# Three query and key buffers, and attention's load buffers laid out as whole weight tiles

## The chip, the cores and the metric

The kernel runs on one core of a Trainium2 chip. The metric is device time in microseconds (us) of one execution; three timed executions of the kernel before gave a median of 371.08 us, and one more was profiled. The names of the engines are those of the profile: PE is the matrix engine, DVE, ACT and POOL are the vector, scalar and general engines, SP is the queue from which nearly every load is issued.

## The reference

Three layers follow each other. Attention over 4 batches, 8 heads, 576 positions and a head size of 64, where a head sees only the last 32 positions (heads 0 to 3) or every 32nd position (heads 4 to 7):

```python
scores = scale * np.matmul(q, k.transpose(0, 1, 3, 2))
scores = np.where(masks[None, :, :, :], scores, -1000000000.0)
attn = softmax(scores);  x = (attn @ v) as 2304 x 512
```

A mixture of 8 experts over 32 slots (4 per expert), with a softmax over all 2304 tokens into the slots and one over the slots out of them:

```python
logits = x @ phi;  d = softmax(logits, axis=0);  slot_input = d.T @ x
slot_out[e] = np.maximum(slot_input[e] @ w1[e], 0) @ w2[e]      # w1: 512x1024, w2: 1024x512
x = softmax(logits, axis=1) @ slot_out
```

And a gated layer: `(silu(x @ w_gate) * (x @ w_val)) @ w_out`, with 1536 hidden units. Its three weights are float64 bit patterns that the kernel converts itself.

## The kernel before, in words

**Attention** is done in 16 units (two batches of one head each), every unit in three steps, 48 steps. The loop goes through them two at a time: in the pass for steps n and n+1 it issues the score products of both (`qk`, L290), the products with v of the steps four back (`pv`, L328), the transposes of the steps two back (`tr`, L315, copied by ACT at L318), and the exponentials (`expo`, ACT at L308) of the two. Transposes of the finished x (L353), the logits (L373) and, for the first eight units, the slot sums (L438) stand between them. Every engine runs its instructions in exactly this written order.

**Loads** go out on SP's queue in written order. Queries and keys of a unit are two loads (`load_qk`, L259 and L260), its values one (`load_v`, L268), after which POOL copies parts of the values (L271). Each has two buffers (`AHEAD = 2`): the pair for unit u+2 is issued after unit u's last score product is issued, the values for u+2 after the last product of unit u with its values. SP waits, in order, for the last reader of the buffer. A table, `WSCHED`, says how many weight halves (128x1024, 512 KB) are issued after each unit by `load_half` (L178). At most eight loads are on their way: every load also waits for the landing of the one eight places ahead of it, and `order` shows that wait by the name of one of eight counters, DMAHW0 to DMAHW7, taken in turn.

**Weights.** There are 70 halves: six of the gated layer's (`PRE`, converted during attention, L194 to L208), 32 of w1 (16 tiles of two halves, tile 2e+h for expert e) and 32 of w2 (tiles 16 to 31). A ring of 15 whole tiles (`NB = 15`, pool `wp`) takes most of them. When attention is over its load buffers (pool `ld`) are given up as a whole, and three further tiles (`wp2`) and the slot input `sz` are placed there. The tiles in `SPEC` and `SPLIT` go into attention's own x buffers and work space as these come free.

**After attention** come the slot sums' rest, then w1 (L644, 16 tiles, in the order `W1ORDER`, each freed ring tile taking the next w2 tile), the hidden units, and w2 (L733, 16 tiles, in the order `W2ORDER`). At the end of w2 the pools are closed and a new pool `fr` is laid over the same memory: four buffers `g` for the gated layer's next weights (`load_g`, L674), the split output weights and the accumulators. A new buffer waits for the last use of every old tile that it covers.

**The gated layer** starts with two prepared weight tiles. Its opening (`HEAD`) is written out by hand: products with tile 0 (`a0`), then ACT takes the first half of the next gate tile from its `g` buffer (L224), then the rest. The long tail is its output products (L840).

Of the kernel before, what the change touches and what calls it, by code (L numbers as in the profile page):

```python
# [17 lines left out]
S = 576  # L18
HD = 64
NT = 9  # L20
# [7 lines left out]
NB = 15  # L28
NB2 = 3
# [3 lines left out]
WORDER = list(range(1, 13)) + list(W2ORDER[:6]) + list(SPEC) + [SPLIT] + list(W2ORDER[6:])  # L33
W1ORDER = (1, 2, 3, 4, 5, 6, 0, 7, 14, 8, 15, 9, 10, 13, 12, 11)
# [22 lines left out]
WSCHED = [2, 2, 2, 2, 2, 2, 2, 2, 2, 2, 5, 3, 2, 2, 1, 2, 3]  # L57
# [4 lines left out]
AHEAD = 2  # L62
# [48 lines left out]
def build(ctx: ExitStack, tc: tile.TileContext, cst, phi, qh, kh, vh, w1, w2, wgv, wo, out):  # L111
# [10 lines left out]
    es_ld = ExitStack()  # L122
    lp = es_ld.enter_context(tc.tile_pool(name="ld", bufs=1, side="right"))
# [15 lines left out]
    qt, kt, vt = [], [], []  # L139
    for j in range(AHEAD):  # L140
        qt.append(lp.tile([128, S], F32, name=f"q{j}"))
        kt.append(lp.tile([128, PAD + S], F32, name=f"k{j}"))
        vt.append(lp.tile([96, 2 * NT * (HD + 1)], F32, name=f"v{j}"))
    col = lp.tile([128, 128], F32, name="col")
    par = lp.tile([128, 16], F32, name="par")
    ml = lp.tile([128, 192], F32, name="ml")
    ms = lp.tile([128, 720], F32, name="ms")

    wsrc = [w1[j] for j in range(16)] + [w2[j] for j in range(16)]
    loads = [(j, hf) for j in PRE + WORDER for hf in range(2)]  # L150
    loads.remove((SPEC[0], 0))
    loads.insert(2 * (NB + len(PRE)), (SPEC[0], 0))
    loads.remove((SPLIT, 0))
    loads.insert(2 * (NB + len(PRE) + NB2) + 1, (SPLIT, 0))
# [4 lines left out]
    def load_half(k, pool=wp, bufs=NB):  # L159
        for _ in range(k):  # L160
# [3 lines left out]
            if j in SPEC:  # L164
                wt[j, hf] = (ap_.tile([128, 1024], F32, tag="xT", name="wx", bufs=1) if hf and j == SPEC[0] else
                             ap_.tile([128, 1024], F32, tag="x", name="wx", bufs=5))
            elif j == SPLIT:
                wt[j, hf] = ap_.tile([128, 1024], F32, tag="eT", name="wx", bufs=1) if hf else tmp[:, 0:1024]
# [10 lines left out]
            wn[0] += 1  # L179

# [75 lines left out]
    def load_qk(u):  # L256
        if u >= 16:
            return
        SP.dma_start(out=qt[u % AHEAD], in_=qh[u])  # L259
        SP.dma_start(out=kt[u % AHEAD][:, PAD:], in_=kh[u])  # L260

    VW = NT * 2 * (HD + 1)

    def load_v(u):
        if u >= 16:
            return
        t = vt[u % AHEAD]
# [716 lines left out]
```

## Time and profile before

| what | us |
|---|---|
| median of three timed executions (369.25, 371.08, 371.54) | 371.08 |
| the profiled execution's own time | 369.73 |
| its span, first to last instruction | 367.9 |
| attention: first score product to last product with v | 5.5 to 105.4 |
| slot sums and slot input | 105 to 121.4 |
| w1 | 121.4 to 135.7 |
| w2 | 137.1 to 156.1 |
| gated layer | 156.1 to 367.9 |

All times below are counted from the start of the span. PE is busy 343.1 us of it (93%). A row of the timeline merges instructions of one line and tells the start, the length from the first start to the last end, the engine, the line, the operation with output and inputs, the count, and in brackets how long the engine stood idle before it and what ended that. Matmul counts are of records: one fp32 product is two.

### The profile page before, as it was taken

What the parts mean: (1) busy time and instruction counts of PE and PEld (TensorE: products, weight loads), DVE (VectorE), ACT (ScalarE), POOL (GpSimd) and SP (SyncE); (2) the same over time, 40 slices, a digit from 0 to 9 for tenths busy, and PEclk for the clock granted to TensorE, in tenths of its full rate; (3) what the DMA queues carried; (4) which work ended last, traced back from release to release, by engine and by line L of the source; (5) the groups of instructions that cost most, each with busy time, mean ns of one, the idle gap of its engine ahead of it and who ended that gap; (6) DMA issues with size and microseconds to landing.
All of it is one profiled execution on the core that took longest, in us unless ns stands there. A gap on an engine that the chain in (4) does not pass through costs nothing.

```text
span 367.9 us, 7753 instructions
## 1 busy us (share of the span) xinstructions
PE 343.1 (93%) x2866; PEld 247.4 (67%) x2866; DVE 219.6 (60%) x705; ACT 186.7 (51%) x448; POOL 130.7 (36%) x161
## 2 busy tenths in 40 slices
PE   7799999899979999989999998999998889999995
PEld 3687776787746543346776776867775577878785
DVE  5568685855636016367787887877768724242432
ACT  3587878767743002356565746544544443333331
POOL 2221232022210020046374848444655544334431
PEclk9889999999989999999999999999999999999999
DMA  8989999998896999963322433233300003030331
GB/s 272 331 260 366 348 364 329 400 370 263 274 362 257 359 411 406 411 254 115 115 83 86 175 116 122 106 116 114 115 2 1 0 2 115 0 117 0 114 114 59
DMA packets 23110, 71.96 MB, mean 196 GB/s; under 512 B 2592, under 2 KB 2976, under 8 KB 23072
## 3 DMA queue, kind: packets, MB, share of 16 engines
q1 hardware_dynamic: 22928, 71.45, 53.3%
q8 instruction: 23, 0.38, 0.4%
q14 instruction: 15, 0.12, 0.1%
q10 hardware_dynamic: 144, 0.01, 0.0%
HBM read 66.73 MB, written 4.72 MB: 194 GB/s over the span
## 4 chain that ended last, share of the span: by engine, by line
PE 62%; DVE 15%; DMA 10%; ACT 7%; issue 3%; POOL 1%; SPq 0%; DVEq 0%; ACTq 0%
PE o L840 30%; DMA k<-in_kh 5%; PE sc L290 5%; PE pv L733 4%; PE pv L328 4%; PE tr L315 3%; PE gv L813 3%; DMA w<-in_w 3%; DVE cv L233 2%; DVE h L820 2%; DVE cv L229 2%; PE gv L814 2%; PE tr L353 2%; PE ms L438 2%; PE lg L373 2%
## 5 line engine op out<-in xcount | busy, mean ns | idle before, releaser
L822 POOL TENSOR_TENSOR hl<-h,hh 128x512 fp32r<-128x512 f32 (+1 forms) x60 | 70.8, 1180 | 93.1 <-ACT hh L821 93.1
L840 PE MATMUL o<-woh,hh 128*128 128x512 f32 (+1 forms) x222 | 87.7, 396 | 2.8 <-DVE acc L866 1.4
L840 PE MATMUL o<-wol,hh 128*128 128x512 f32 (+1 forms) x222 | 85.4, 386 | 0.0
L820 DVE TENSOR_TENSOR h<-gv,sg 128x512 f32<-128x512 f32 (+1 forms) x59 | 37.5, 636 | 56.7 <-ACT sg L819 51.8
L821 ACT CAST hh<-h 128x512 fp32r<-128x512 f32 (+1 forms) x60 | 34.7, 578 | 56.9 <-DVE h L820 56.0
L840 PE MATMUL o<-woh,hl 128*128 128x512 f32 (+1 forms) x222 | 59.4, 385 | 0.0
L840 PEld LDWEIGHTS o<-woh,hh 128*128 128x128 f32 x222 | 41.7, 188 | 17.4 <-DVE osb L866 3.0
L271 POOL COPY v<-v 32x390 f32<-32x390 f32 (+1 forms) x48 | 22.4, 499 | 75.7 <-DMA v<-in_vh 44.3
L840 PEld LDWEIGHTS o<-woh,hl 128*128 128x128 f32 x222 | 41.4, 188 | 8.5
L840 PEld LDWEIGHTS o<-wol,hh 128*128 128x128 f32 x222 | 41.8, 188 | 7.6
L819 ACT ACTIVATE sg<-gv 128x512 f32<-128x512 f32 (+1 forms) x60 | 33.3, 555 | 24.8 <-PE gv L813 24.4
L308 ACT ACTIVATE tmp<-tmp,mx 128x96 f32<-128x96 f32 (+1 forms) x144 | 40.8, 362 | 5.2 <-DVE mx L296 5.2
L290 PE MATMUL sc<-k,q 64*64 64x96 f32 (+1 forms) x576 | 29.3, 250 | 4.5 <-DMA k<-in_kh 3.0
L290 PEld LDWEIGHTS sc<-k,q 64*64 64x64 f32 x576 | 24.6, 140 | 13.0 <-issue 6.7
L318 ACT COPY tmp<-tr 96x384 f32<-96x384 f32 x47 | 20.3, 477 | 21.8 <-PE tr L315 21.7
L813 PE MATMUL gv<-cs,St 128*128 128x512 f32 (+1 forms) x60 | 25.4, 424 | 4.0 <-DVE St L802 4.0
L784 POOL TENSOR_TENSOR wol<-wo,woh 128x512 fp32r<-128x512 f32 x12 | 15.5, 1291 | 21.7 <-DMA g<-in_wgv 21.0
L328 PE MATMUL pv<-v,tmp 96*64 96x65 f32 x576 | 23.1, 230 | 0.0
L814 PE MATMUL gv<-cs,St 128*128 128x512 f32 (+1 forms) x59 | 22.2, 376 | 0.2 <-DVE h L820 0.2
L315 PE MATMUL tr<-cst_t,tmp 128*96 128x128 f32 x144 | 21.7, 287 | 0.5 <-ACT xT L354 0.5
L328 PEld LDWEIGHTS pv<-v,tmp 96*64 96x64 f32 x576 | 19.7, 141 | 3.6 <-issue 2.1
L233 DVE SCALAR_TENSOR_TENSOR cv<-g,cv 128x512 int32<-128x512 int32 x30 | 20.8, 692 | 0.7
(164 smaller groups left out, 468.8 us busy)
## 6 DMA issues: line engine op xcount, KB each, us to landing
w<-in_w SPq DMA_DIRECT2D x56, 512.0 KB, 7.4
g<-in_wgv SPq DMA_DIRECT2D x10, 1024.0 KB, 5.0
g<-in_wo SPq DMA_DIRECT2D x5, 1024.0 KB, 5.0
v<-in_vh SPq DMA_DIRECT2D x16, 292.5 KB, 5.0
q<-in_qh SPq DMA_DIRECT2D x16, 288.0 KB, 5.0
k<-in_kh SPq DMA_DIRECT2D x16, 288.0 KB, 5.6
out<-osb SPq DMA_DIRECT2D x17, 256.0 KB, 2.2
wx<-in_w SPq DMA_DIRECT2D x7, 512.0 KB, 4.5
```

The costliest lines, as they stand in the source:

```text
L233: DVE.scalar_tensor_tensor(out=cv[0], in0=v[:, :, 0], scalar=29, in1=cv[0], op0=ALU.logical_shift_right, op1=ALU.bitwise_or)
L290: PE.matmul(out=ps[r, W * j:W * j + W], lhsT=qt[u % AHEAD][r, 64 * i:64 * i + 64], rhs=kt[u % AHEAD][r, c0:c0 + W], start=True, stop=True, ...
L308: ACT.activation(out=e[:, j, 96 - W:96], in_=sm[:, j, 0:W], func=AF.Exp, scale=-1.0, bias=mx[:, j:j + 1])
L315: PE.transpose(ps[0:96, 128 * j:128 * j + 128], e[:, j, :], ident)
L328: PE.matmul(out=ps[64 * b:64 * b + 64, o:o + 65], lhsT=a[:, j, 64 * b:64 * b + 64], rhs=vt[u % AHEAD][:, 65 * (NT * b + 3 * t + j):65 * (N ...
L813: PE.matmul(out=pg[:, 0:n], lhsT=St[f][:, 0:128], rhs=csf[:, t0:t0 + n], start=True, stop=True)
L814: PE.matmul(out=pvv[:, 0:n], lhsT=St[f][:, 128:256], rhs=csf[:, t0:t0 + n], start=True, stop=True)
L819: ACT.activation(out=sg[:, 0:n], in_=pg[:, 0:n], func=AF.Silu)
L820: DVE.tensor_tensor(out=h[:, 0:n], in0=pvv[:, 0:n], in1=sg[:, 0:n], op=ALU.mult)
L821: ACT.copy(hh[bi, f][:, 0:n], h[:, 0:n])
L822: POOL.tensor_tensor(out=hl[bi, f][:, 0:n], in0=h[:, 0:n], in1=hh[bi, f][:, 0:n].bitcast(F32), op=ALU.subtract)
L840: PE.matmul(out=o[:, 0:c], lhsT=(a, a, l)[i][:, 128 * t:128 * t + 128], rhs=(woh, wol, woh)[i][f][:, c * k:c * k + c], start=(first and i ...
```

## The change

Queries and keys get three buffers (`QAHEAD`), values keep two (`VAHEAD`). The buffers no longer lie in separate tiles: they are slices of three whole weight tiles, sA, sB and sC, and of a smaller sD. The ring has 14 tiles. When the last reader of sB, sA or sC is done, that tile takes one w2 tile (`SHARED`: 20, 22, 24), so these loads are issued before attention ends. sD becomes the slot input. The pool of the four is closed only together with the ring. A weight half's place in the order of loads, the table of how far the loads are to have come after each unit (`WTO`, counted from the first) and `W1ORDER` are new, and the values, queries, keys and weights of a unit are now issued in one place, behind the unit's last product with v. x gets six buffers for five.

```diff
-NB = 15
-NB2 = 3
+NB = 14
-WORDER = list(range(1, 13)) + list(W2ORDER[:6]) + list(SPEC) + [SPLIT] + list(W2ORDER[6:])
-W1ORDER = (1, 2, 3, 4, 5, 6, 0, 7, 14, 8, 15, 9, 10, 13, 12, 11)
+SHARED = W2ORDER[2:5]
+WORDER = list(range(1, 13)) + list(W2ORDER[:2])
+REST = list(W2ORDER[5:])
+W1ORDER = (1, 2, 3, 4, 0, 13, 5, 6, 7, 14, 8, 15, 9, 10, 12, 11)
...
-WSCHED = [2, 2, 2, 2, 2, 2, 2, 2, 2, 2, 5, 3, 2, 2, 1, 2, 3]
+WTO = [6, 8, 10, 12, 14, 16, 18, 20, 22, 24, 26, 29, 33, 38, 42, 43]
-AHEAD = 2
+QAHEAD = 3
+VAHEAD = 2
...
-    lp = es_ld.enter_context(tc.tile_pool(name="ld", bufs=1, side="right"))
+    lp = es_w2.enter_context(tc.tile_pool(name="ld", bufs=1, side="right"))
...
+    sB, sA, sC = shared = [lp.tile([128, 2048], F32, name=f"s{n}") for n in "BAC"]
+    sD = lp.tile([128, 1890], F32, name="sD")
+    VW = NT * 2 * (HD + 1)
+    qt = [sA[:, 0:576], sA[:, 1184:1760], sB[:, 608:1184]]
+    kt = [sA[:, 576:1184], sB[:, 0:608], sB[:, 1184:1792]]
+    vt = [sC[0:96, 0:VW], sD[0:96, 0:VW]]
...
+    loads = halves(*PRE, *WORDER, SPEC[0], *SHARED, SPLIT, *SPEC[1:], *REST)
...
-                a = pool.tile([128, 2048], F32, tag="w", name="w", bufs=bufs)
+                a = shared[SHARED.index(j)] if j in SHARED else wp.tile([128, 2048], F32, tag="w", name="w", bufs=NB)
...
+    def load_to(m):
+        load_half(m - wn[0])
...
         load_v(1)
-        load_half(WSCHED[0])
+        load_qk(2)
+        load_half(2)
...
                     qk(u, t)
-                    if t == 2:
-                        load_qk(u + AHEAD)
+            if n == 2:
+                load_qk(3)
+                load_half(2)
...
                     if t == 2:
-                        load_v(u + AHEAD)
+                        load_v(u + VAHEAD)
+                        load_qk(u + 4)
+                        load_to(WTO[u])
                         if u == 15:
-                            load_half(2 * (NB + len(PRE)) + 1 - wn[0])
-                            es_ld.close()
...
+                            szt.append(sD[:, 0:1152].rearrange("p (c k) -> p c k", c=4))
                             POOL.memset(szt[0], 0.0)
...
-            for k in two:
-                if k % 3 == 2 and k < len(steps):
-                    u = k // 3
-                    load_half(min(WSCHED[u + 1], 2 * (NB + (len(PRE) if u > 11 else 0)) + (u > 12) - wn[0]))
```

SP's queue at the start, before (q_78, k_79 and v_80 are the first buffers, q_81, k_82 and v_83 the second; w<-in_wgv are halves of the prepared gate tiles):

```order
L259 DMA q_78<-in_qh 128x576
L260 DMA k_79<-in_kh 128x576
L268 DMA v_80<-in_vh 64x1170
L259 DMA q_81<-in_qh 128x576
L260 DMA k_82<-in_kh 128x576
L523 DMA phi_t<-in_phi 128x128
L268 DMA v_83<-in_vh 64x1170
L178 DMA w<-in_wgv 128x1024 x2
L259 DMA q_78<-in_qh 128x576
L260 DMA k_79<-in_kh 128x576
```

and now (sA, sB hold queries and keys, sC, sD values):

```order
L263 DMA sB<-in_kh 128x576
L524 DMA phi_t<-in_phi 128x128
L269 DMA sD<-in_vh 64x1170
L262 DMA sB<-in_qh 128x576
L263 DMA sB<-in_kh 128x576
L178 DMA w<-in_wgv 128x1024 x2
L262 DMA sA<-in_qh 128x576
L263 DMA sA<-in_kh 128x576
L178 DMA w<-in_wgv 128x1024 x2
L269 DMA sC<-in_vh 64x1170
```

Queries and keys of unit 2 stand ahead of the first two weight halves, in buffers that nothing has used.

SP's queue late in attention, before, from the last queries and keys (unit 15) to the loads behind attention (wx and tmp are halves in attention's x buffers and work space):

```order
L259 DMA q_81<-in_qh 128x576
L260 DMA k_82<-in_kh 128x576
L178 DMA w<-in_w 128x1024
L268 DMA v_80<-in_vh 64x1170
L268 DMA v_83<-in_vh 64x1170
L178 DMA w<-in_w 128x1024 x3
L178 DMA wx<-in_w 128x1024
L178 DMA w<-in_w 128x1024 x6
L178 DMA tmp<-in_w 128x1024
L178 DMA wx<-in_w 128x1024 x6
L178 DMA w<-in_w 128x1024 x20
```

and now, from right behind the last queries and keys:

```order
L178 DMA w<-in_w 128x1024 x3
L269 DMA sC<-in_vh 64x1170
L178 DMA w<-in_w 128x1024 x4
L269 DMA sD<-in_vh 64x1170
L178 DMA w<-in_w 128x1024
L178 DMA wx<-in_w 128x1024 x2
L178 DMA sB<-in_w 128x1024 x2
L178 DMA sA<-in_w 128x1024 x2
L178 DMA sC<-in_w 128x1024 x2
L178 DMA tmp<-in_w 128x1024
L178 DMA wx<-in_w 128x1024 x5
L178 DMA w<-in_w 128x1024 x22
```

Four weight halves now stand between the values of unit 14 and those of unit 15 where none stood, and 22 halves are left for the time behind w1's start where 20 were.

SP's queue at the end of the weights, with the counters that each load waits for, before:

```order
L178 DMA w<-in_w 128x1024 [waits DMAHW6_49,PE_49]
L178 DMA w<-in_w 128x1024 [waits DMAHW7_49]
L674 DMA g<-in_wgv 128x2x1024 [waits DMAHW0_49,PE_49]
L674 DMA g<-in_wgv 128x2x1024 [waits DMAHW1_49]
L674 DMA g<-in_wo 128x2x1024 [waits DMAHW3_49,DMAHW2_49,PE_49]
```

and now:

```order
L178 DMA w<-in_w 128x1024 [waits DMAHW6_49,PE_49]
L178 DMA w<-in_w 128x1024 [waits DMAHW7_49]
L670 DMA g<-in_wgv 128x2x1024 [waits DMAHW0_49,DMAHW6_49,DVE_49,DMAHW7_49,PE_49,Pool_49]
L670 DMA g<-in_wgv 128x2x1024 [waits DMAHW5_49,DMAHW4_49,DMAHW1_49]
L670 DMA g<-in_wo 128x2x1024 [waits DMAHW2_49]
```

The first g load now waits also for the two weight halves right ahead of it (DMAHW6, DMAHW7), since its buffer covers the tile that they fill. In the built program the value of its PE wait is the count at the last product of w2's tenth tile before, and at the last product of the sixteenth and last tile now.

## Rows read from the trace of the kernel before

**Rows 1.** The page: granted clock in 40 slices, loads with KB and us to landing.

```profile
PEclk9889999999989999999999999999999999999999
...
w<-in_w SPq DMA_DIRECT2D x56, 512.0 KB, 7.4
...
v<-in_vh SPq DMA_DIRECT2D x16, 292.5 KB, 5.0
```

**Rows 2.** Who waited for whom, PE, 0 to 110 us: total, times, longest.

```profile
PE sc L290 <- DMA k<-in_kh: 3.0, 3, 2.0
```

**Rows 3.** Timeline of PE, 9 to 25 us.

```profile
12.15 0.86 PE L315 MATMUL tr<-cst_t,tmp 128*96 128x128 f32 x6
15.04 1.87 PE L290 MATMUL sc<-k,q 64*64 64x80 f32 x24 [2.03 <-DMA k<-in_kh]
...
18.33 1.52 PE L315 MATMUL tr<-cst_t,tmp 128*96 128x128 f32 x6
```

**Rows 4.** Timeline of ACT, 9 to 25 us.

```profile
13.47 1.70 ACT L308 ACTIVATE tmp<-tmp,mx 128x96 f32<-128x96 f32 x6
19.25 0.47 ACT L318 COPY tmp<-tr 96x384 f32<-96x384 f32 x1 [4.08 <-PE tr L315]
```

**Rows 5.** Timeline of PE, 22 to 110 us.

```profile
24.33 1.05 PE L290 MATMUL sc<-k,q 64*64 64x80 f32 x24
...
31.98 0.71 PE L290 MATMUL sc<-k,q 64*64 64x96 f32 x12 [0.43 <-DMA k<-in_kh]
...
36.99 1.23 PE L328 MATMUL pv<-v,tmp 96*64 96x65 f32 x24
...
46.62 1.05 PE L290 MATMUL sc<-k,q 64*64 64x80 f32 x24
...
54.47 0.71 PE L290 MATMUL sc<-k,q 64*64 64x96 f32 x12 [0.55 <-DMA k<-in_kh]
...
101.53 0.92 PE L328 MATMUL pv<-v,tmp 96*64 96x65 f32 x24
```

**Rows 6.** Stretches: busy us of each engine, granted clock, share and GB/s of the loads.

```profile
14.00:22.00 8.00, 6.96 (x92) 6.13 (x94) 3.38 (x30) 3.76 (x14) 0.00 (x0) 0.57 0.84 318
...
32.00:55.00 23.00, 21.97 (x370) 17.11 (x370) 18.21 (x108) 18.49 (x59) 5.97 (x12) 1.00 0.98 359
...
137.00:158.00 21.00, 20.89 (x175) 8.22 (x175) 10.34 (x31) 6.63 (x11) 0.86 (x1) 1.00 1.03 409
```

**Rows 7.** Timelines of SP and POOL around the last two loads of values.

```profile
92.95 3.50 SPq L268 DMA_DIRECT2D v<-in_vh  x2
...
99.20 1.31 POOL L271 COPY v<-v 32x260 f32<-32x260 f32 x3 [1.45 <-DMA v<-in_vh]
```

**Rows 8.** Chain of waits around w1: start, us, what.

```profile
121.53 5.53 DMA wx<-in_w
```

**Rows 9.** Tile w, issues from 143.4 us: the last weight half and its landing.

```profile
L178 SPq DMA_DIRECT2D w<-in_w x1: 328/328/328, 143.4 to 143.4; - x1
...
DMA to landing us min/median/max: 10.5/10.5/10.5
```

**Rows 10.** Timeline of PE, 119 to 162 us.

```profile
121.39 5.69 PE L644 MATMUL sc<-w,sz 128*32 128x512 f32 x47
...
154.17 1.92 PE L733 MATMUL pv<-w,hz 128*32 128x512 f32 x16
```

**Rows 11.** Timeline of SP, 59 to 165 us.

```profile
148.33 0.90 SPq L674 DMA_DIRECT2D g<-in_wgv  x2
```

**Rows 12.** Tile g: us from issue to landing, 15 loads of 1 MB.

```profile
DMA to landing us min/median/max: 4.8/5.0/10.3
```

**Rows 13.** Timeline of all engines, 155 to 170 us.

```profile
156.16 0.37 ACT L747 COPY so<-pv 128x256 f32<-128x256 f32 x1 [5.50 <-PE pv L733]
...
159.11 0.70 ACT L224 ACTIVATE wg<-g 128x512 f32<-128x512 f32 x1
...
161.75 0.50 PE L813 MATMUL gv<-cs,St 128*128 128x512 f32 x1 [0.23 <-DVE St L802]
```

More of the change, by code (lines that the diff above doesn't have):

```diff
@@ L137, in build, with halves @@
     s_sb = cp.tile([64, 2], F32, name="s_sb")
[L139 to L147, printed above, removed]
-    wsrc = [w1[j] for j in range(16)] + [w2[j] for j in range(16)]
[L150 to L154, printed above, removed]
+    sB, sA, sC = shared = [lp.tile([128, 2048], F32, name=f"s{n}") for n in "BAC"]
[4 more added lines that the diff above has]
+    vt = [sC[0:96, 0:VW], sD[0:96, 0:VW]]
+    col, par = sA[:, 1760:1888], sA[:, 1888:1904]
+    ml, ms = sB[:, 1792:1984], sD[:, VW:VW + 720]
+    wsrc = [w1[j] for j in range(16)] + [w2[j] for j in range(16)]
+    def halves(*js):
+        return [(j, hf) for j in js for hf in range(2)]
+    loads = halves(*PRE, *WORDER, SPEC[0], *SHARED, SPLIT, *SPEC[1:], *REST)
+    at_spec = loads.index((SPEC[0], 0))
+    at_split = loads.index((SPLIT, 0))
     wt, gt = {}, {}
@@ L157, in build, with load_half @@
     NW = len(loads)
-    def load_half(k, pool=wp, bufs=NB):
+    def load_half(k):
         for _ in range(k):
@@ L164, in load_half @@
             if j in SPEC:
-                wt[j, hf] = (ap_.tile([128, 1024], F32, tag="xT", name="wx", bufs=1) if hf and j == SPEC[0] else
-                             ap_.tile([128, 1024], F32, tag="x", name="wx", bufs=5))
+                wt[j, hf] = ap_.tile([128, 1024], F32, tag="x", name="wx", bufs=6)
             elif j == SPLIT:
-                wt[j, hf] = ap_.tile([128, 1024], F32, tag="eT", name="wx", bufs=1) if hf else tmp[:, 0:1024]
+                wt[j, hf] = ap_.tile([128, 1024], F32, tag="xT", name="wx", bufs=1) if hf else tmp[:, 0:1024]
             elif hf == 0:
-                a = pool.tile([128, 2048], F32, tag="w", name="w", bufs=bufs)
+                a = shared[SHARED.index(j)] if j in SHARED else wp.tile([128, 2048], F32, tag="w", name="w", bufs=NB)
                 if j in PRE:
@@ L258, in load_qk @@
             return
-        SP.dma_start(out=qt[u % AHEAD], in_=qh[u])
-        SP.dma_start(out=kt[u % AHEAD][:, PAD:], in_=kh[u])
-    VW = NT * 2 * (HD + 1)
+        SP.dma_start(out=qt[u % QAHEAD], in_=qh[u])
+        SP.dma_start(out=kt[u % QAHEAD][:, PAD:], in_=kh[u])
     def load_v(u):
@@ L266, in load_v @@
             return
-        t = vt[u % AHEAD]
+        t = vt[u % VAHEAD]
         SP.dma_start(out=t[32:96], in_=vh[u])
@@ L289, in qk @@
                 r = slice(64 * b, 64 * b + 64)
-                PE.matmul(out=ps[r, W * j:W * j + W], lhsT=qt[u % AHEAD][r, 64 * i:64 * i + 64],
-                          rhs=kt[u % AHEAD][r, c0:c0 + W], start=True, stop=True, skip_group_check=True)
+                PE.matmul(out=ps[r, W * j:W * j + W], lhsT=qt[u % QAHEAD][r, 64 * i:64 * i + 64],
+                          rhs=kt[u % QAHEAD][r, c0:c0 + W], start=True, stop=True, skip_group_check=True)
         o = 288 * ((3 * u + t) % 2)
@@ L340, in pv @@
             if t == 0 and e == 0:
-                xt[bp, y, st] = ap_.tile([128, NT, 128], F32, tag="x", name="x", bufs=5)
+                xt[bp, y, st] = ap_.tile([128, NT, 128], F32, tag="x", name="x", bufs=6)
             DVE.tensor_tensor(out=xt[bp, y, st][:, 3 * t:3 * t + m, 64 * e:64 * e + 64], in0=p3[:, n:n + m, 0:HD],
@@ L513, in build @@
         POOL.iota(col, pattern=[[1, 128]], base=0, channel_multiplier=0, allow_small_or_imprecise_dtypes=True)
-        for j in range(AHEAD):
+        for j in range(QAHEAD):
             e = DVE if j == 0 else POOL
             e.memset(kt[j][:, 0:PAD], 0.0)
-        for j in range(AHEAD):
+        for j in range(VAHEAD):
             POOL.memset(vt[j].rearrange("p (b i d) -> p b i d", b=2, i=NT)[0:32, :, 0, :], 0.0)
```

11 lines of the change are left out of this document (3 added, 8 removed).

## The prediction

> **What bounds the kernel now.** I read the page first, then PE's waits during attention, then the timelines of PE and ACT where those waits stand, then the busy time by stretches, and last the places behind attention at which a load is late.
>
> The page shows the granted clock down to 8 tenths in slices 2 and 3, from 9 to 28 us, and in slice 12, around 106 us [rows 1]; elsewhere it is full. PE waits for keys three times in attention, 3.0 us in all, the longest 2.0 us [rows 2]. That longest wait ends at 15.04 us, when the keys of unit 2 land. In the stretch 14 to 22 us the granted clock averages 0.57 of full [rows 6], which means that nearly all of it is spent at 1.2 instead of 2.4 GHz: PE had stood idle for 2.03 us, and the same six transposes that took 0.86 us at 12.15 take 1.52 us at 18.33 [rows 3]. So one late load costs its wait and, behind it, a stretch at half speed.
>
> Later in attention PE has hardly a gap: two waits for keys of 0.43 and 0.55 us and one product group with late values that takes 1.23 instead of 0.92 us [rows 5]. Attention is bound by PE, and the load stream runs right beside it: at 32 to 55 us the loads keep their engines 98% busy at 359 GB/s [rows 6].
>
> Behind attention w1 and w2 are packed on PE, and the loads run at 409 GB/s [rows 6]; the last weight half is issued at 143.4 and lands 10.5 us later, at 153.9 [rows 9], while PE starts w2's last two tiles at 154.17 [rows 10]. The gated layer's next tile is issued at 148.33 [rows 11], and ACT takes it at 159.11 [rows 13].
>
> **The start of attention.** Queries and keys of unit 2 now need no buffer to come free and stand ahead of two weight halves, so the wait of 2.03 us goes. The cover for the two delayed halves: the conversion that reads them is done by ACT only behind its exponentials of steps 6 and 7. On PE, the granted clock lacks 0.43 of 8 us from 14 to 22 [rows 6], 3.4 us of full speed; less what fell into the idle time before 15.04, some 3.0 us of work were lost, as the score group's 1.87 for 1.05 us and the transposes' 1.52 for 0.86 tell [rows 3, 5]. PE alone would gain 2.0 + 3.0 = 5.0 us. But ACT is next: it ends its exponentials at 13.47 + 1.70 = 15.17 and copies the next transposes at 19.25, idle for 4.08 us [rows 4]. Those transposes need these exponentials, so ACT can come forward by 4.08 us less the time from an exponential's end to a copy, roughly a triple of transposes, 0.3 us: **3.8 us**. The bounds are 2.0 (the clock falls all the same) and 5.0.
>
> **The other waits for keys.** With a third buffer the loads for a unit go out a unit earlier; 0.43 + 0.55 us go, and the 0.31 us of late values at 36.99 [rows 5] if the values are in time. I count **1.1 us** of the 1.29; bounds 0 and 1.3.
>
> Whether the stream follows: a unit loads 288 + 288 + 292.5 KB and two halves of 512 KB [rows 1], 1.938 MB; at 359 GB/s that is 5.40 us. Four units take 46.62 - 24.33 = 22.29 us on PE, less the waits of 0.43 and 0.31 some 5.39 us each [rows 5]. The two are equal. Values keep two buffers and now stand first in a unit's group of loads, in front of its own weights, but behind the weights of the unit before. So the gain stands, with nothing to spare.
>
> **The values of unit 15.** Four weight halves now stand between the last two loads of values. Before, SP issued those two together from 92.95 on, and POOL could copy the second at 99.20; PE needs it in the second half of the group at 101.53 [rows 5, 7], about 102.0. Now: values of unit 14 land some 3 us behind 92.95 (the second load, issued by 96.45, took no more), four halves at 409 GB/s are 5.1 us, the values 0.7 more and POOL's first copy 0.4: 102.2 to 103.3, by how far earlier weights still queue. That is a new wait of 0.2 to 1.3 us on PE near attention's end, all of it on the path: I take **0.6 us** lost.
>
> **w1 and w2.** Both are PE's, and shift with attention's end. 22 halves follow w1's start in place of 20, but one fewer stands ahead of them. Before, the last of those ahead landed at 121.53 + 5.53 = 127.06 [rows 8] and 20 more took until 153.9, 1.34 us each. Now, on the same scale, they begin at 125.7 and end at 125.7 + 22 x 1.34 = 155.2. The second half of the last tile is used at about 155.6 (a quarter of the 1.92 us before the end of the group at 154.17 [rows 10]). Covered by 0.4 us; bounds 0 and 1 us lost. The Trainium skill (DMA: Bandwidth & Descriptors, Specifications) puts the limit of one core's reading at about 358 GB/s. By that figure 22 halves would take 32.2 us, end at 157.9, and w2 would end 2.3 us later; the row of 409 GB/s in this stretch speaks against it.
>
> **The first load of the gated layer.** This is the change's price. Its buffer covers the ring tile that w2's last tile is in, so it waits for w2's last product, where it went out at 148.33 before [rows 11], at the tenth tile. ACT's copy behind that last product starts at 156.16 [rows 13]; SP can issue at about 156.15. With nothing ahead of it a 1 MB load takes 4.8 to 5.0 us [rows 12]: it lands at 161.1. ACT reaches it at 159.11 and stands in order before the copies that both first St tiles need, so it waits 2.0 us, and PE's first product of the layer at 161.75 [rows 13] comes 2.0 us later. What is queued behind ACT is the whole opening; no other work fills it. **2.0 us** lost; bounds 1.8, and 5 if the clock falls in the longer pause. The loads behind it land 2.6 us apart and are used later than that.
>
> **Sum.** -3.8 - 1.1 + 0.6 + 0 + 2.0 = -2.3 us against the profiled execution of 369.73: 367.4. That execution lies 1.35 us under the median of 371.08, on whose scale the sum is 368.8. I say 368.3, between them and nearer to the median's.
>
> **Rivals.**
> - *The front gain is PE's whole.* If ACT's part can be caught up within the next units (it is busy 18.49 of 23 us at 32 to 55 us [rows 6]), the front gives 5.0 + 1.3 us, and if the values of unit 15 come in time nothing is lost there: -6.3 + 2.0 = -4.3, 366 with the same scale. Against it: ACT's copies gate PE's next groups. Chance 0.22.
> - *The wait moves from keys to values.* In the first units keys of units 2 and 3 are now ahead of the values of unit 3; if those come 2 us late PE idles as long as before and the clock falls all the same. Then only about 1 us is left of the front: -1 + 0.6 + 2.0 = +1.6, about 372. For it: the balance of 5.40 against 5.39 us. Against it: values of a unit are needed two pairs of steps after their issue. Chance 0.13.
> - *The stream falls behind, and the kernel is slower.* At the 318 GB/s of 14 to 22 us [rows 6] a unit's loads take 6.1 us, 0.7 more than PE's unit; through units 2 to 9 PE would wait 8 x 0.7 = 5.6 us for values, which takes the whole front gain and 0.7 more, with 0.6 and 2.0 us behind attention and one more fall of the clock of 3 us as at 15 us: +6.3, about 376. It decides from the point where a unit's loads take longer than 5.4 us. Against it: that stretch had a paused stream (84% share [rows 6]). Chance 0.10.
> - *The loads behind attention run no faster than those within it.* At 359 GB/s [rows 6] the 22 halves take 32.1 us and end at 157.8, 2.2 us behind their use: 370.5. Chance 0.03, since the stretch from 137 us shows 409 GB/s. The figure of the page named above would do the same.
> - *The third buffer does nothing*, because slices of one tile wait for each other: the front would give nothing, and the rest +2.6, 373. In the program the score products name only the counters of their own loads. Chance 0.02.
>
> **The numbers.** The forecast as worked out has a chance of 0.50, with 366 to 370.5 as its own range. Faster by over 1% is below 367.4, slower above 374.8; 1% is about what a measurement of this kernel tells from no change. Faster: four fifths of the first rival (0.18) and a quarter of the forecast (0.12), 0.30. Slower: the stream's rival (0.10) and the upper end of the moved wait (0.04), 0.14. Same: 0.56. The range from 364.5 to 373.0 leaves out the stream's rival and the outermost ends of the others.
>
> **What would show it.** Right, if the changed kernel's profile has no wait of PE for keys, a full clock from 14 to 22 us and ACT idle for well under 1 us there; if PE waits for values only once, below 1.3 us, shortly before attention's end; if attention ends 4 to 5 us earlier; if the first g load is issued right at w2's end and ACT waits about 2 us for it. Wrong, if PE idles for values in several units, if the clock is low in another stretch, if the last weight halves land behind w2's last tile, or if ACT meets its g tile in time.

## The result, and the profile after

The changed kernel is slower: median 374.13 us of 10 runs (372.58 to 379.01) against 370.69 of 10 runs of the kernel before (368.74 to 372.68), ratio 1.0103 with a 95% interval of 1.0063 to 1.0144. One run of the changed kernel, at 379.01 us, lies over 1.5% above the fastest and is left out of the ratio, as such runs are in the ratios and the mean times at half clock below. Forecast was 368.3, 0.7% under the 371.08 known then. The profiled execution has a span of 372.8 us against 367.9.

The page's granted clock, in 40 slices, shows at once what was right and what was not: the start is at full clock where [rows 1] had 8 tenths, and attention's end (slice 12, from 102.5 us) is worse than before, 5 tenths for 8.

```profile
PEclk9999999999959999999999999999999999999999
```

PE's timeline at the start, 9 to 25 us (start, us, engine, line, operation; in brackets the idle time before and who ended it):

```profile
12.60 0.86 PE L316 MATMUL tr<-cst_t,tmp 128*96 128x128 f32 x6
13.38 1.05 PE L291 MATMUL sc<-sB 64*64 64x80 f32 x24
...
17.83 0.86 PE L316 MATMUL tr<-cst_t,tmp 128*96 128x128 f32 x6
19.67 0.55 PE L354 MATMUL tr<-cst_t,x 128*128 128x128 f32 x3 [0.98 <-ACT tmp L319]
...
20.48 1.05 PE L291 MATMUL sc<-sA 64*64 64x80 f32 x24
```

These answer to [rows 3, 5]: no wait for keys, transposes at 0.86 us throughout, the scores of steps 10 and 11 at 20.48 instead of 24.33. The next engine is ACT, as forecast: PE waits for it 0.98 us, and ACT's idle time behind the exponentials of steps 4 and 5, 4.08 us in [rows 4], is 0.17 us now:

```profile
15.78 0.85 ACT L319 COPY tmp<-tr 96x384 f32<-96x384 f32 x2 [0.17 <-PE tr L316]
```

Between the start and attention's end PE waits twice for values. Each of the two product groups (`pv`) falls into two parts, the second behind the wait:

```profile
25.33 0.57 PE L329 MATMUL pv<-sC,tmp 96*64 96x65 f32 x12
26.14 0.88 PE L329 MATMUL pv<-sD,tmp 96*64 96x65 f32 x12 [0.23 <-DMA sD<-in_vh]
26.95 0.86 PE L316 MATMUL tr<-cst_t,tmp 128*96 128x128 f32 x6
...
47.60 0.57 PE L329 MATMUL pv<-sC,tmp 96*64 96x65 f32 x12
49.04 0.89 PE L329 MATMUL pv<-sD,tmp 96*64 96x65 f32 x12 [0.87 <-DMA sD<-in_vh]
49.86 0.86 PE L316 MATMUL tr<-cst_t,tmp 128*96 128x128 f32 x6
```

From the start of such a group to the transposes behind it, it takes 0.85 us where nothing is late, and 1.62 and 2.26 us here.

The end of attention on SP's queue and on PE. First the loads, 88 to 104 us (start, us of the issues, destination, count); the last load of values, at 92.57, took 8.5 us to land:

```profile
89.63 0.52 SPq L269 DMA_DIRECT2D sC<-in_vh  x1
90.20 2.00 SPq L178 DMA_DIRECT2D w<-in_w  x4
92.57 0.52 SPq L269 DMA_DIRECT2D sD<-in_vh  x1
```

Then PE, 94 to 125 us, and two stretches of it (busy us of each engine, granted clock, load share, GB/s):

```profile
95.91 0.92 PE L329 MATMUL pv<-sC,tmp 96*64 96x65 f32 x24
...
101.21 1.14 PE L329 MATMUL pv<-sD,tmp 96*64 96x65 f32 x12 [2.46 <-DMA sD<-in_vh]
102.27 1.52 PE L316 MATMUL tr<-cst_t,tmp 128*96 128x128 f32 x6
...
105.19 1.57 PE L329 MATMUL pv<-sD,tmp 96*64 96x65 f32 x24
...
123.05 2.36 PE L640 MATMUL sc<-w,sD 128*32 128x512 f32 x18
```

```profile
95.00:101.00 6.00, 3.75 (x69) 2.63 (x63) 2.06 (x15) 3.87 (x13) 0.50 (x1) 1.00 1.03 408
101.00:111.00 10.00, 7.57 (x59) 5.11 (x59) 2.35 (x8) 1.91 (x4) 2.37 (x4) 0.51 1.02 409
```

PE stands idle for 2.46 us until the values of unit 15 land, and what follows runs at 1.2 GHz for the next ten microseconds (granted clock 0.51): transposes 1.52 instead of 0.86 us. From the group at 95.91 to w1's first product it takes 27.1 us. The same group in the trace of the kernel before:

```profile
99.26 0.92 PE L328 MATMUL pv<-v,tmp 96*64 96x65 f32 x24
```

That is 22.1 us to w1's start at 121.39 [rows 10]. So 5.0 us are lost here, more than the start had won.

Behind attention, all engines, 155 to 170 us, against [rows 10, 11, 13]:

```profile
155.83 2.77 PE L729 MATMUL pv<-w,hz 128*32 128x512 f32 x16
...
158.65 0.37 ACT L743 COPY so<-pv 128x256 f32<-128x256 f32 x1 [6.35 <-PE pv L729]
158.68 0.90 SPq L670 DMA_DIRECT2D g<-in_wgv  x2
...
163.63 0.66 ACT L227 ACTIVATE wg<-g 128x512 f32<-128x512 f32 x1 [1.92 <-DMA g<-in_wgv]
...
166.23 0.50 PE L809 MATMUL gv<-cs,St 128*128 128x512 f32 x1 [0.93 <-DVE St L798]
```

The first g load is issued 0.03 us behind ACT's copy of w2's result, and ACT waits 1.92 us for it. The last two tiles of w2 take 2.77 us where they took 1.92. The weight loads of the products with the last half (PEld is PE taking a weight tile in) show why, before and after:

```profile
155.06 0.13 PEld L733 LDWEIGHTS pv<-w,hz 128*32 128x32 f32 x4 [0.30 <-issue]
```

```profile
157.55 0.14 PEld L729 LDWEIGHTS pv<-w,hz 128*32 128x32 f32 x4 [0.72 <-DMA w<-in_w]
```

Before, they start 33.67 us behind w1's start and wait for no load; now they start 34.50 us behind it, when the last half has landed.

Between the two profiled executions the 4.9 us add up like this (later is +): scores of steps 10 and 11 at -3.85; from there to the group at 95.91 +0.50; from it to w1's start +5.01; w1 and w2 +0.86; from w2's last product (155.50, now 158.01) to the gated layer's first +1.97; the gated layer +0.42.

### The profile page after: what moved, and what is told of

Read it like the earlier page. It is cut to its first block, busy times and chain, and to the rows that moved or that the text cites. A ratio compares the mean times of both kernels' runs of the same rounds, so it can differ in the third digit from the quotient of the medians.

```text
span 372.8 us, 7710 instructions
## 1 busy us (share of the span) xinstructions
PE 344.5 (92%) x2866; PEld 246.6 (66%) x2866; DVE 219.7 (59%) x705; ACT 186.1 (50%) x448; POOL 131.2 (35%) x162
## 4 chain that ended last, share of the span: by engine, by line
PE 71%; DVE 11%; DMA 9%; ACT 6%; issue 2%; POOL 0%; DVEq 0%; SPq 0%; ACTq 0%; POOLq 0%
PE o L836 33%; DMA sD<-in_vh 7%; PE sc L291 5%; PE pv L329 4%; PE pv L729 4%; PE sc L640 4%; PE tr L316 3%; PE gv L809 3%; PE gv L810 3%; DVE cv L236 2%; DVE h L816 2%; PE ms L439 2%; PE gv L789 2%; PE lg L374 1%; DVE cv L232 1%
## 5 line engine op out<-in xcount | busy, mean ns | idle before, releaser
L272 POOL COPY sC<-sC 32x390 f32<-32x390 f32 (+1 forms) x24 | 12.5, 520 | 44.3 <-DMA sC<-in_vh 29.4
L272 POOL COPY sD<-sD 32x390 f32<-32x390 f32 (+1 forms) x24 | 10.4, 467 | 32.8 <-DMA sD<-in_vh 32.8
L297 DVE CUSTOM_DVE_ANT_0 tmp<-sc,sD 128x80 f32<-128x80 f32 x72 | 14.1, 238 | 8.6 <-PE sc L291 7.8
L809 PEld LDWEIGHTS gv<-cs,St 128*128 128x128 f32 x60 | 11.3, 188 | 11.7 <-DVE St L798 4.7
L297 DVE CUSTOM_DVE_ANT_0 tmp<-sc,sB 128x96 f32<-128x96 f32 x72 | 14.3, 253 | 6.5 <-PE sc L291 5.1
```

Of the source, the lines that this page charges most:

```text
L272: POOL.tensor_copy(t4[0:32, :, i0:i1, :], t4[64:96, :, i0 - 1:i1 - 1, :])
L297: DVE.tensor_tensor_reduce(out=sm[:, j, 0:W], in0=ps[:, W * j:W * j + W], in1=mask(y, 3 * t + j), scale=-0.125, scalar=3.0e38, op0=ALU.add ...
L809: PE.matmul(out=pg[:, 0:n], lhsT=St[f][:, 0:128], rhs=csf[:, t0:t0 + n], start=True, stop=True)
```

## The experiments

Times at half clock in this section are worked out from each run's mean granted clock as 2 x (1 - clock) x span; "before" there is the kernel before run beside the experiment. Within the 29 of these runs beside e1 to e4 that count in the ratio, the span grows by 0.31 us per us at half clock, within all 35 by 0.42. A warm matmul is a product on PE whose result nothing uses.

**e1: the values of unit 15 ahead of the four weight halves.**

```diff
-WTO = [6, 8, 10, 12, 14, 16, 18, 20, 22, 24, 26, 29, 33, 38, 42, 43]
+WTO = [6, 8, 10, 12, 14, 16, 18, 20, 22, 24, 26, 29, 29, 38, 42, 43]
```

> The changed kernel with one number changed: the four weight halves that unit 12 issues (halves 29 to 32) are issued behind the values of unit 15 instead of ahead of them. Theory 1 (the lost 5.0 us between pv of step 46, at 95.9 us, and w1's first product, at 123.0, are the 2.46 us that PE waits for these values and the half clock of 101.1 to 111.4 us behind that wait): the values land about 4.5 us after their issue at 92.6, that is near 97, before their pv at 98.8; the wait of 2.46 us goes, the granted clock stays full through the tail of attention, pv of step 46 to w1's start takes 22 to 23 us as in the kernel before (22.1) instead of 27.1, and the run is 4 to 5 us shorter than the changed kernel: 369 to 370, ratio to before 0.995 to 1.0. Rival A (the tail's clock falls by itself, since ACT and DVE hold PE there): only the wait goes, 1.5 to 2.5 us, and the half clock stays: 372, ratio 1.003. Rival B (the stream of weights is what is late): w1's start stays near 123 since the halves come 2.4 us later, and nothing is gained.

(The "pv of step 46" there is the group at 95.91, which the loop issues at its step 46.) Measured: median 370.62, ratio 1.0036 (1.0003 to 1.0068). SP's load and PE's timeline:

```profile
91.66 0.51 SPq L269 DMA_DIRECT2D sD<-in_vh  x1
```

```profile
97.65 0.52 PE L329 MATMUL pv<-sD,tmp 96*64 96x65 f32 x12
...
104.94 3.72 PE L509 MATMUL ms<-warm_t 128*128 128x512 bf16 x10
...
117.44 1.07 PE L640 MATMUL sc<-w,sD 128*32 128x512 f32 x6
```

The load lands after 3.3 instead of 8.5 us, the wait is gone, and from the group that now starts at 94.99 to w1's start it takes 22.45 us. A shorter half clock stays, over the warm matmuls (3.72 us for ten where 2.3 to 2.4 us is their time at full clock), as in the kernel before. In the profile w1 starts 5.6 us earlier; by the ratios the edit is worth 0.67%, 2.5 us. Theory 1 holds for the place: at 95 to 101 and 101 to 111 us the granted clock is 1.00 and 0.83, where the changed kernel has 1.00 and 0.51. It overstates the size in ordinary runs, whose ratio is nearer to rival A's 1.003 than to its own 0.995 to 1.0. e2 below, with the changed kernel's order of loads, waits 1.69 us in its profile, not 2.46:

```profile
99.16 0.89 PE L329 MATMUL pv<-sD,tmp 96*64 96x65 f32 x12 [1.69 <-DMA sD<-in_vh]
```

**e2: the four g buffers behind the other tiles of their pool**, so that they cover ring tiles that w2 reads early.

```diff
-        for _ in range(NG):
-            load_g(fr, "g", NG)
         St = [fl.tile([128, 256], F32R, name=f"St{f}") for f in range(12)]
...
         acc = [fr.tile([128, 512], F32, name=f"acc{t}") for t in range(18)]
+        for _ in range(NG):
+            load_g(fr, "g", NG)
```

> The changed kernel with the four buffers of the gated layer's first loads allocated behind that layer's other right-side tiles, so that they lie over weight tiles that w2 has read early and not over the tile that it reads last; nothing else changes, no instruction moves. Theory 1 (g0's issue at 158.7 is set by its wait for w2's last product): g0 is issued at about 149, right behind the weight halves, and lands about 2.6 us after the last of them, near 160.1 instead of 163.5, g1 near 162.7 instead of 167.4; the gated layer starts 1.3 to 2.4 us earlier and the run is that much shorter: 371.7 to 372.8, ratio to before 1.003 to 1.006. Rival (loads of 1 MB side by side with the last halves only delay these: the bandwidth is shared): the last half lands later than 157.5, w2 ends later, and less than 0.5 us is gained: 374.

Measured: 373.45, ratio 1.0055 (1.0021 to 1.0089), 0.48% or 1.8 us better than the changed kernel. Two of its timelines, SP and PE:

```profile
145.35 1.85 SPq L670 DMA_DIRECT2D g<-in_wgv  x2
```

```profile
152.88 2.70 PE L729 MATMUL pv<-w,hz 128*32 128x512 f32 x16
...
161.21 0.50 PE L809 MATMUL gv<-cs,St 128*128 128x512 f32 x1 [0.21 <-DVE St L798]
```

From w2's last product to the gated layer's first it is 6.22 us, as in the kernel before (6.25), instead of 8.22. The wait cost 1.97 us, where the forecast had 2.0. The last weight halves are not delayed by the loads behind them: the two tiles take 2.70 us against 2.77.

**e3: both edits.**

> Both edits of the two runs before together. Theory 1: the gains add, since one lies before w1's start and the other behind w2's end: 5.3 to 7.4 us less than the changed kernel, 366.7 to 368.8, and 1 to 4 us less than the kernel before, ratio 0.990 to 0.995. What is left to the kernel before is then the start's 3.9 us less what the longer stream of weights costs (the last half 1 us too late for w2, g0 some 1 us later behind w2's end). Rival A with the tail's own clock fall: 369.5 to 371, ratio about 1.0.

Measured: 369.70, ratio 0.9950 (0.9913 to 0.9987), 1.5% or 5.7 us against the changed kernel. The two gains alone make 2.5 + 1.8 = 4.3 us; by the ratios the order of loads is worth 3.9 us from e2 to e3 and the place of the g buffers 3.2 from e1 to e3, and the intervals leave this open. The kernel is now 1.9 us faster than the one before by the ratio, less than the 2.35 us by which its gated layer starts earlier in the profile (159.40 against 161.75). In that profile the difference lies in the gated layer, PE and one stretch near 290 us:

```profile
293.69 0.79 PE L809 MATMUL gv<-cs,St 128*128 128x512 f32 x1 [3.00 <-DVE St L798]
294.29 0.63 PE L810 MATMUL gv<-cs,St 128*128 128x512 f32 x1
```

```profile
292.00:300.00 8.00, 6.31 (x15) 4.98 (x16) 1.37 (x3) 2.11 (x4) 2.80 (x3) 0.57 0.00 1
```

Every kernel of this case waits 3.0 us there; in this execution the clock fell behind it and the gated layer took 209.3 us, against 206.6 in the changed kernel's. In the two executions first compared it did not fall.

**e4: PE kept busy through the wait for unit 15's values** (changed kernel).

```diff
             a = at.pop((u, t))
+            if (u, t) == (15, 0):
+                warm(10)
```

> The changed kernel with ten warm matmuls (2.41 us at full clock, no result used) put on PE between the two halves of the pv that waits for unit 15's values: the wait stays, but PE works through it. It tells the wait from the clock. Theory 1: the granted clock does not fall at 101.1 us; the values still land near 101.1, and the tail behind them runs at full clock, as in the kernel before: of the 5.0 us lost, 2 to 3 come back, 371 to 372, ratio 1.001 to 1.004. Rival A (the clock falls whatever PE does there, since the waits behind follow in any case): half clock from about 102, nothing back or up to 0.5 us lost, 374 to 374.6. Rival C (the clock's fall is harmless since ACT and DVE set the pace of the tail): the clock stays full and the time does not move, 374.

Measured: 373.35, ratio 1.0087 (1.0050 to 1.0123), so 0.6 us back by the ratios where theory 1 had 2 to 3, and the intervals leave open whether it is any. PE:

```profile
98.22 2.33 PE L511 MATMUL ms<-warm_t 128*128 128x512 bf16 x10
100.48 0.57 PE L331 MATMUL pv<-sD,tmp 96*64 96x65 f32 x12
...
162.86 1.09 PE L798 MATMUL o<-asb,cst_t 128*128 128x256 f32 x2 [2.35 <-ACT asb L794]
164.49 0.80 PE L811 MATMUL gv<-cs,St 128*128 128x512 f32 x1 [0.53 <-DVE St L800]
```

The clock stays full through the wait (granted clock 1.00 from 98 to 104 us), and the group behind takes 0.57 us, so the fall at 101 us was due to the idle time; the profile of e12, with the same filling, has no fall there either, and that of e2, without it, has one. But g0's wait now leaves PE idle for 2.35 us at 162.9, and the clock falls there, for some 7 us. A fall that is taken away in one place may come in the next gap.

**e5 and e9: two buffers of queries and keys on the shared tiles.**

> The kernel with both edits (e3_both), but with two buffers of queries and keys again, each pair loaded behind the last scores of the unit that used its buffer, as in the kernel before; the shared tiles stay. It measures what the third buffer alone is worth. Theory 1 (the start's gain and the missing waits for keys come from the third buffer): PE waits some 2 us for keys at step 6 again, and shortly at later units; scores of steps 10 and 11 start near 24 instead of 20.5 to 21 us; w1's first product comes 3.5 to 5 us later than in e3_both (118.2), near 122 to 123; in the runs 3 to 4.5 us more than e3_both, 372.5 to 374, ratio to before 1.003 to 1.009. Rival (the gain at the start comes from the other order of loads, or is made up later in any case): no change from e3_both, ratio 0.995.

In e5 unit 15's keys lay in a tile that the weights overwrite before its last scores are taken, and PE waited 14.2 us for weights there; its 389.93 says nothing of the third buffer. e9 mends this, on the basis of e8 (below):

```diff
-    qt = [sA[:, 0:576], sA[:, 1184:1760], sB[:, 608:1184]]
-    kt = [sA[:, 576:1184], sB[:, 0:608], sB[:, 1184:1792]]
+    qt = [sA[:, 1184:1760], sA[:, 0:576]]
+    kt = [sB[:, 0:608], sA[:, 576:1184]]
...
                     qk(u, t)
+                    if t == 2 and u > 0:
+                        load_qk(u + 2)
...
```

(`QAHEAD` is 2. Of the changed kernel's calls, `load_qk(2)` ahead of the loop and `load_qk(u + 4)` go, and `load_qk(3)` becomes `load_qk(2)`.)

> The kernel e8_no_idle with two buffers of queries and keys instead of three, each pair loaded behind the last scores of the unit that used its buffer, as in the kernel before; unit 15's keys lie in the tile that the weights take last. All else as in e8_no_idle (367.4 us, no time at half clock). It measures the third buffer alone. Theory 1 (the waits for keys and the clock's fall behind the first are what the third buffer removes): PE waits about 2 us for keys at step 6 and 0.8 to 1.3 us in all at later units, half clock behind step 6 in those runs in which it falls (1.8 to 2.1 us more); scores of steps 10 and 11 start near 24 us instead of about 21; w1's first product 3 to 5 us later than in e8_no_idle (118.9); run 370 to 372, ratio to before 0.998 to 1.004. Rival (half of the gain at the start is made up later in any case, by waits for ACT and for the weights): run 368 to 369, ratio 0.993 to 0.996.

Measured: 374.37, ratio 1.0100 (1.0065 to 1.0134), 1.9% or 7.0 us slower than e8, more than either theory said. PE's waits up to 110 us (in total, times, longest):

```profile
PE sc L291 <- DMA sA<-in_kh: 4.6, 3, 2.2
...
PE sc L291 <- DMA sB<-in_kh: 1.7, 1, 1.7
```

All 6.3 us are waits for keys, and e8 has none. They are more than in [rows 2] (3.0 us). The loads here stand in another order than in the kernel before, and that kernel's own waits differ from one execution to the next (3.0 to 5.8 us, below); which of the two makes the difference, no run tells. So the 7.0 us are what the third buffer is worth on the shared tiles with this order, not what it gave the kernel before.

**e6: PE kept busy through the first wait of the kernel before.**

```diff
                     u, t = steps[k]
+                    if k == 6:
+                        warm(9)
                     qk(u, t)
```

> The kernel before with nine warm matmuls (some 2.2 us at full clock, no result used) on PE ahead of the scores of step 6, where it waits 2.03 us for keys of unit 2. The wait stays; it tells what part of the start's 3.85 us was the clock. Theory 1 (wait 2.0, the half clock of 14.8 to 21.6 behind it the other 1.8): no fall of the granted clock at the start; scores of steps 10 and 11 start at 22.3 to 22.8 us instead of 24.3. In the runs of the kernel before the start's fall (about 6.6 us at half clock) shows in about 17 of 29 by their mean granted clocks, and the runs with it are 1.9 us longer; so the mean gain is about 1 us, ratio 0.996 to 0.999, and the mean time at half clock goes from 6.1 us to 2 to 3. Rival A (ACT sets the pace there, the clock costs nothing): 24.3 as before, ratio 1.000. Rival B (the clock falls in any case): half clock still there.

```profile
13.02 2.11 PE L508 MATMUL ms<-warm_t 128*128 128x512 bf16 x9
15.05 1.05 PE L290 MATMUL sc<-k,q 64*64 64x80 f32 x24
...
22.19 1.05 PE L290 MATMUL sc<-k,q 64*64 64x80 f32 x24
```

The scores of step 6 start where they did [rows 3], those of steps 10 and 11 2.14 us earlier [rows 5]. So the start's 3.85 us divide into a wait and some 2 us of clock. The runs, at ratio 0.9993 (0.9962 to 1.0025), show no gain where about 1 us was expected, and cannot exclude one.

**e7: e3 without the last weight half** (w2's last tile uses its first half twice).

```diff
             wn[0] += 1
+            if wn[0] == NW - 1:
+                wt[j, 1] = wt[j, 0]
+                wn[0] = NW
```

> The kernel with both edits (e3_both), less the last load of w2: the second half of its last tile is not loaded and the products take the tile's first half twice (this part of w2 is left out). It tests whether the last half landing is what ends w2. From w1's first product to w2's last product start: 34.1 us in the kernel before, 35.0 in the changed kernel and in e1, e2 and e3 (34.9 to 35.2). Theory 1 (w2 ends when the last of 22 halves has landed): 34.1 to 34.2, with the last landed half ahead of the product that reads it, and g0 lands 1.3 us earlier against w1's start. Rival (the products or DVE's transposes between them set the pace): 35.0.

```profile
117.58 3.98 PE L643 MATMUL sc<-w,sD 128*32 128x512 f32 x31
...
150.36 1.92 PE L732 MATMUL pv<-w,hz 128*32 128x512 f32 x16
```

The last two tiles take 1.92 us again, as in [rows 10], and from the start of w1's first to that of w2's last product it is 34.11 us, as in the kernel before, instead of 34.97 in the changed kernel. So the wait for the last half sets w2's end, and costs 0.86 us.

**e8, e11 and e12: no gap left in which the clock falls.** e8 is e3 with 18 warm matmuls where PE idles in every kernel here; e11 is the kernel before with the same and those of e6; e12 is the changed kernel with the same and those of e4.

```diff
+        if (bp, y, st) == (1, 1, 1):
+            warm((2, 4, 0)[t], ("sc", 2))
         ps = bank(*bk)
...
         a = xT.pop((bp, y, st))
+        if bp and last:
+            warm(2, ("sc", 2))
...
                 force(n, ("g", seq[n][2]))
+                if n == 38:
+                    warm(10, ("gv", 3))
```

> The kernel with both edits (e3_both), with 18 warm matmuls at places where PE idles in every kernel of this case: two, four and two ahead of the last unit's transposes and logits (idle 0.57, 1.09 and 0.62 us) and ten in the gated layer where PE waits 3.0 us for DVE's St (near 292 us). Theory (what separates runs of one kernel is how often the clock falls behind these gaps; each us at half clock costs some 0.3 us over all runs): the mean time at half clock goes from 6.7 us in e3_both to 4 or less, and the mean run is 0.8 to 1.5 us shorter than e3_both: ratio to before 0.990 to 0.993. Rival A (the falls come in any case): half clock as in e3_both, 6 to 7 us, ratio 0.995. Rival B (the warm matmuls delay what stands behind them by as much as they give): half clock less, ratio 0.995 all the same.

> The kernel before with the warm matmuls of e8_no_idle at the same places, and with the nine of e6_warm_start at the start: the kernel before without the clock's falls. It tells what the changed tiles and loads are worth when the clock stays full in both. Theory 1: mean time at half clock under 1.5 us instead of 6 to 8; 2.0 to 2.5 us slower than e8_no_idle (at step 6 the wait of 2.0 us is still there, later waits for keys 0.8; against that w2 does not wait for its last half, 0.9): 369.4 to 370, ratio to before 0.996 to 0.998. Rival (what the runs of the kernel before suggest when their spans are set against their time at half clock, 366.1 us at none): 367.9, ratio 0.992, the third buffer then worth 0.5 us or less at full clock.

> The changed kernel with the same 18 warm matmuls and with the ten of e4_warm_tail in the wait for unit 15's values: the changed kernel without the clock's falls, its two waits still in it. Theory 1: mean time at half clock under 2 us instead of 12.7; slower than e8_no_idle by the wait for the values (1.7 to 2.5 us, filled with warm matmuls) and by g0's wait for w2's last product (2.0): 3.7 to 4.5 us, 371.1 to 372, ratio to before 1.001 to 1.004, so that the clock's falls were 2 to 3 us of the changed kernel's 374.1. Rival (the falls of the clock were nearly all of the loss): 368 to 369, ratio 0.994 to 0.996.

| kernel | median us | ratio to before | mean us at half clock |
|---|---|---|---|
| e8, both edits | 367.44 | 0.9911 (0.9879 to 0.9943) | 0.4 (e3: 6.7) |
| e11, kernel before | 368.26 | 0.9935 (0.9904 to 0.9966) | 0.9 (without: 6.1 to 8.2) |
| e12, changed kernel | 372.21 | 1.0039 (1.0006 to 1.0073) | 5.2 (without: 12.7) |

PE in e8 near 290 us, to be held against e3:

```profile
291.18 2.32 PE L513 MATMUL gv<-warm_t 128*128 128x512 bf16 x10
294.35 0.50 PE L813 MATMUL gv<-cs,St 128*128 128x512 f32 x1 [0.85 <-DVE St L802]
```

The product group starts as far behind the start of the gated layer (134.3 us in both) and runs at full clock. e8 is the fastest version, 0.9% ahead of the kernel before. From e12 to e8 it is 1.28%, 4.7 us, somewhat above the 3.7 to 4.5 expected for the two waits alone; some falls were left in e12. From e11 to e8 it is 0.24%, 0.9 us, and the two intervals overlap: with the clock kept up in both, the kernel before is hardly behind. Here the rival of e11 came nearer than theory 1. From e11 to e12, the two kernels of this case with the gaps filled, it is 1.04%, 3.9 us, as much as without the filling. But e12 is left with 5.2 us at half clock and e11 with 0.9, so how much of the loss in ordinary runs is the clock's stays open.

**Four more profiles of the kernel before.**

> The kernel before, unchanged, profiled once more (first of four looks): whether the granted clock falls behind the wait for keys at step 6. Theory 1 (a chance of the execution): in two or fewer of the four looks half clock at 15 to 22 us, the others at full clock there, with scores of steps 10 and 11 near 22 to 22.5 instead of 24.3 us. Rival (it falls each time, and the gain is made up later): half clock there in three or four of the four.

> Second look at the kernel before: as for the first. The wait itself (about 2 us at step 6) is there each time by either.

> Third look at the kernel before: as for the first. Half clock at attention's tail or in the gated layer near 290 us may come or not by either theory.

> Fourth look at the kernel before: as for the first, with half clock at 15 to 22 us in it or not.

The granted clock of the first two, whose scores of steps 10 and 11 start at 22.83 and 25.47, and of the third (24.87), which the fourth (24.50) repeats digit for digit:

```profile
PEclk9999999999989999999999999999999989999999
```

```profile
PEclk9969989999998999999999999999999989999999
```

```profile
PEclk9989999999999999999999999999999999999999
```

The clock falls at the start in three of the four, as the rival said; but not behind step 6, where those three wait 0.2 to 0.9 us; the longer wait is now at step 9, for the keys of unit 3, 2.2 to 3.3 us. The first, with waits of 1.6 and 1.5 us, keeps its clock. In five executions PE waits 3.0 to 5.8 us for keys, and the scores of steps 10 and 11 start at 24.4 us in the mean; in the changed kernel and in e3 and e8 they start at 20.4 to 20.5. The gain of the start was no chance of one execution. At attention's end the clock falls in three of the five, in the gated layer in two.

## Why the prediction was wrong

**The start of attention** was right: 3.8 us forecast, 3.85 in the profile pair and 3.9 against the mean of five, ACT next in line. That the clock was part of it is shown by e6. The place of the wait, though, was that of one execution: in three of the four further profiles the long wait comes at step 9.

**The other waits for keys** were forecast at 1.1 us and gave nothing. The waits went, but from the scores of step 10 to the group at 95.91 it took 75.4 us against 74.9. Waits for values of units 3 and 7, 0.23 at 26.1 and 0.87 us at 49.0, took their place, as the rival of the moved wait had it; the clock did not fall with them. The groups in which they fall also run slower behind the wait, so that the two lose 0.77 and 1.41 us, 2.2 in all. The two groups with late keys and the one with late values before lost 0.65, 0.78 and 0.31 us, 1.7 in all. That is 0.44 of the 0.50. The step that failed here is the condition on which the 1.1 us stood, that values are in time with nothing to spare.

**The values of unit 15** are the step that failed, and the larger part of the miss: forecast +0.6, bounds 0.2 to 1.3; measured 2.46 us of waiting and, to w1's start, 5.0. Two things were wrong. The landing was built from two durations that were both too short: the values of unit 14 took 4.2 us to land and not 3, and three weight halves issued before them were still under way (they landed at 90.7, 91.9 and 93.2); and from there to the landing of unit 15's values it was 7.2 us (93.9 to 101.1) and not 5.8, the first of the four halves landing 2.7 us behind the values of unit 14. That is 2.6 us more than in the sum. The 0.4 us of POOL's first copy were not on the path, since PE starts at 101.21, 0.1 us behind the landing; so the wait is 0.2 + 2.6 - 0.4 = 2.4 us, as measured. And the wait was priced as a wait alone, although the same text had just worked out for 15 us what a gap of 2.0 us does to the clock. That e1 takes the wait and the ten microseconds at half clock away together, and e4 the fall alone, shows both parts. In ordinary runs the step costs 2.5 us (changed kernel to e1) to 3.9 us (e2 to e3), less than the 5.0 of this one profile and four times the forecast or more.

**w1 and w2** were forecast at nothing, with a cover of 0.4 us; they lost 0.86. The last half landed 34.46 us behind w1's start, where 33.8 was forecast, and it is needed earlier than I took it: where nothing is late the products with it start 33.67 us behind w1's start (155.06 in the trace of the kernel before, 0.43 us behind the first ones of their tile), and not 34.2 (155.6). So the cover of 0.4 us was a lack of 0.1 in the forecast's own terms, and the later landing makes it 0.8. The rate was nearly right, 22 halves from 127.43 to 157.51, 1.37 us each against 1.34. By the limit of the Trainium skill (DMA: Bandwidth & Descriptors, Specifications), about 358 GB/s, they would take an estimated 32.2 us; the trace has 30.1 us, and 409 GB/s in the stretch of 101 to 111 us, so here the measurement decides: the figure was no limit for this one core.

**The first load of the gated layer** was right: 2.0 us forecast, 1.97 in the profile, 1.8 by the ratios of e2 (3.2 from e1 to e3), through the wait for w2's last product.

**The sum** had -2.3 us against a profile pair that shows +4.9 in span. Of the miss of 7.2 us, 4.4 belong to unit 15's values, 1.6 to the other waits, 0.9 to w1 and w2, 0.4 to the gated layer. By number the nearest rival was the useless third buffer (373, chance 0.02), by accident, since the front did gain what was forecast. By mechanism it was the moved wait, at 372 and a chance of 0.13, but it put the wait into the first units. None of the rivals had a wait with a fall of the clock at attention's end, although both prices stood in the text.

**What is left of the start's gain, and what stays open.** e8 leads e11 by 0.9 us only, with the scores of steps 10 and 11 at 20.5 against 22.9 us. In the two profiles that lead can be followed. It is 2.36 us there. Four product groups with late values then cost e8 1.00, 1.14, 0.54 and 0.66 us; the first two are:

```profile
26.38 0.88 PE L329 MATMUL pv<-sD,tmp 96*64 96x65 f32 x12 [0.46 <-DMA sD<-in_vh]
...
49.01 0.89 PE L329 MATMUL pv<-sD,tmp 96*64 96x65 f32 x12 [0.60 <-DMA sD<-in_vh]
```

Late groups and waits of e11 give back 1.9, so that 0.92 is left at w1's start (118.92 against 119.84). The last half of w2 takes 0.8 of it, and the gated layers start 0.16 us apart (160.03 and 160.19). So with three buffers of queries and keys it is the values, which kept two, that PE waits for; whether a third buffer of values or another order of loads would end this, no run tells. Whether the clock falls in the gated layer is settled in no run here: it did in the profiles of e1, e2, e3, e4, e6 and e7, not in that of the changed kernel, and in two of five of the kernel before.

## What to carry to other kernels

A load that is handed a new place in an in-order queue is priced by everything that the queue still holds at its issue, not by the loads that the change moves alone. Wherever a change opens a gap on PE, count the gap and the half clock that may follow it together. Filling the gap with matmuls can take away the half clock, but not the wait (e4), and the next gap may then bring it. And a buffer that is placed over old tiles waits for the last reader of each tile under it: let the first buffer needed lie over the tile that is free first.

## What the runs showed of the hardware

The clock's fall is a matter of single executions. The same 3.0 us wait in the gated layer is followed by half clock in some profiles of a kernel and not in others, and over the 35 runs of the kernel before beside e1 to e4 the time at half clock ranges from 0 to 17.2 us. Matmuls without a use, in the gaps, brought it to 0.4 us in e8 and made the runs more alike (366.48 to 368.36). One of the gaps filled was 0.57 us long, one 1.09: whether these alone would have let the clock fall, no run tells apart. Alone, this filling made the kernel before 0.65% faster (e11), more than the 0.24% by which e8 then leads it.
